# A fused layer-norm, state-space and Mish feed-forward block on one core: a new order of work, a rotation-table scan, one activation per tile and one weight ring

## The chip, the cores and the metric

The kernel runs on one core of one Trainium2 chip. The time is the device time of that core in microseconds (us), and lower is better. An execution is "fast" when it lies within 1.5% of the fastest of the same kernel, "slow" when it lies above, and "unknown" when there is only one run to judge by. The engines are called PE (TensorE, matmuls), PEld (its weight loads), DVE (VectorE), ACT (ScalarE), POOL (GpSimd) and SP (SyncE, which issues most of the transfers).

## The reference

The input is 2048 rows of 1024 bf16 numbers. The rows are normalised, and the result goes through two branches, which are added to the input.

```python
xn = _layernorm(x)                               # x: 2048 x 1024
# branch A: a diagonal complex recurrence over the rows, P = 1024 states
Lam_bar = jnp.exp(dt * Lam)
B_bar = ((Lam_bar - 1.0) / Lam)[:, None] * Bmat
Bu = jnp.einsum("bld,pd->blp", x + 0j, B_bar)
for t in range(L):
    h = Lam_bar[None, :] * h + Bu[:, t, :]
y = 2.0 * jnp.einsum("blp,dp->bld", hseq, Cmat).real + x * Dskip
# branch B: a feed-forward layer, F = 3584
h = jnp.einsum("bsd,df->bsf", x, w1) + b1
act = h * jnp.tanh(softplus(h))                  # Mish  (softplus is written out in the original)
B = jnp.einsum("bsf,fd->bsd", act, w2)
return x + A(xn) + B(xn)
```

Both kernels work on four blocks of 512 rows. A block has four stages on PE: B (the real and imaginary parts of Bu, 128 matmuls), FFN1 (224), FFN2 (224) and C (128). Every matmul has a 128x128 stationary operand and 512 columns. This makes 704 matmuls per block and 2816 in all, in both kernels. The recurrence itself runs on DVE, with one "scan unit" for each of eight groups of 128 states.

## The kernel before

Its activation takes three passes on ACT, a bias add on DVE before them and a product on POOL after them.

```python
def ffn1_block(c_, pump=None, ln_rts=()):
    for f in range(NF):                          # 28 tiles
        ...                                      # 8 matmuls into banks[bank]
        vop(lambda e, ...: e.tensor_scalar(hb[:, hs, :], banks[bank][:, :], b1col[:, f:f + 1], None, op0=ALU.add), ...)
        if pump is not None:
            ...                                  # block 0: the next pieces of the V tables, on DVE
        aop(lambda e, ...: e.activation(actT[:, f, :], hb[:, hs, :], AF.Exp), ...)
        if f % GRP == GRP - 1 or f == NF - 1:
            ...                                  # AF.Ln for all tiles of the group, then for each of them:
            aop(lambda e, ff=ff: e.activation(actT[:, ff, :], actT[:, ff, :], AF.Tanh), ...)
            pop(lambda e, ...: e.tensor_tensor(actT[:, ff, :], hb[:, hs2, :], actT[:, ff, :], op=ALU.mult), ...)
```

The end of a block makes the residual on POOL, from x and xn that are fetched again from DRAM through four buffers (NXT = 4), while the scan runs on DVE:

```python
def tail_block(c_):
    for j in range(NJ):
        scan_unit(c_, j)                         # 2 scans, carry, 6 bf16 products and sums of 128x512
    for u in range(NU):                          # 8 output tiles
        dma_unit_tiles(c_, u)                    # xtf <- x, xntf <- xn_scr, buffer u % NXT
        xdsk_prep(u)                             # POOL: xdsk = xntf * dsk, then xdsk += xtf
    ...                                          # FFN2, then C with C transposed afresh (dma_rs) in every block
    if c_ + 1 < NB:
        dma_xnT(c_ + 1)                          # 8 transposing loads from xn_scr
    for u in range(NU):
        vop(lambda e, ...: e.tensor_tensor(outs[:, os_, :], banks[u][:, :], xdsk[:, u, :], op=ALU.add), ...)
        ...
```

The start is layer norm of four row tiles, a write of xn to DRAM, eight transposing loads of it, then W1 and the sixteen transposes of B, all on SP's queue. The main loop does B first.

```python
for rt in range(min(NQ, NRT)):
    ln_tile(rt)                                  # load x, normalise, write xn_scr
dma_xnT(0)
for g in range(min(NW1S, NFG)):
    dma_w1(0, g)
for ci, Bsrc in enumerate([A_B_re, A_B_im]):
    for k in range(NK):
        ...                                      # dma_start_transpose(BT[:, ci, k, :], ...)
...
for c_ in range(NB):
    ...
    but_block(c_)                                # stage B
    ...
    ffn1_block(c_, ...)
    ...
    tail_block(c_)                               # scan, residual, FFN2, C, output
```

Of the kernel before, what the change touches and what calls it, by code (L numbers as in the profile page):

```python
# [166 lines left out]

def bass_parallel_sum__ssm_conv_s5__dense_activation_mish__prompt_kernel(
    nc: bass.Bass,
    A_x: bass.AP,  # L170
    A_Lambda_re: bass.AP,
    A_Lambda_im: bass.AP,
    A_B_re: bass.AP,
    A_B_im: bass.AP,
    A_C_re: bass.AP,
    A_C_im: bass.AP,
    A_log_dt: bass.AP,
    A_Dskip: bass.AP,
    B_x: bass.AP,
    B_w1: bass.AP,  # L180
    B_b1: bass.AP,
    B_w2: bass.AP,
    out: bass.AP,
):
    build_kernel(nc, A_x, A_Lambda_re, A_Lambda_im, A_B_re, A_B_im, A_C_re, A_C_im,
                 A_log_dt, A_Dskip, B_w1, B_b1, B_w2, out)


def build_kernel(nc, A_x, A_Lambda_re, A_Lambda_im, A_B_re, A_B_im, A_C_re, A_C_im,
                 A_log_dt, A_Dskip, B_w1, B_b1, B_w2, out, GRP=7, HBR=14):  # L190
    bf16, f32, i32 = DT.bfloat16, DT.float32, DT.int32
    assert len(A_x.shape) == 3 and len(out.shape) == 3
# [4 lines left out]
    assert S % TB == 0 and D % TB == 0 and Pch % P128 == 0 and F % 256 == 0  # L197
    NB = S // TB
    NK = D // P128
    NJ = Pch // P128  # L200
    NF = F // P128
    NFG = NF // 2
    NQ = TB // P128
    NBH = D // TB
    NU = NQ * NBH
    assert NU <= 8
    NRT = S // P128
    NST = D // 512
    GRP = min(GRP, NF)
    HBR = max(GRP, min(HBR, NF))  # L210
    EPS = 1e-5
    TTAB = TB
    LOGT = int(round(math.log2(TTAB)))
    assert (1 << LOGT) == TTAB

    def xrows(r0, nrows):
        return A_x[0, r0:r0 + nrows, :]
# [6 lines left out]

    def dsem(name, nper=1):
        return DmaSem(nc, name, nper)

    final_sem_totals = []

    xn_scr = nc.dram_tensor("bass_xn_scratch", (S, D), bf16).ap()  # L230
# [3 lines left out]

    actT = sb("actT", [P128, NF, TB], bf16); b_act = [Buf("act%d" % f) for f in range(NF)]
    hb = sb("hb", [P128, HBR, TB], bf16); b_hb = [Buf("hb%d" % i) for i in range(HBR)]
    hT = sb("hT", [P128, 2, NJ, TB], bf16); b_hT = [Buf("hT%d" % j) for j in range(NJ)]
    mtmp = sb("mtmp", [P128, 2, TTAB], bf16); b_m = [Buf("m%d" % k) for k in range(2)]
    cum = sb("cum", [P128, 2, TTAB], bf16); b_cum = [Buf("cum%d" % k) for k in range(2)]
    NW2S = 3  # L240
    w2s = sb("w2s", [P128, NW2S, 2, D], bf16); b_w2s = [Buf("w2s%d" % i) for i in range(NW2S)]
    NRS = 4
    rhs = sb("rhs", [P128, NRS, 2, D], bf16); b_rhs = [Buf("rhs%d" % i) for i in range(NRS)]
    NXD = 8
    xdsk = sb("xdsk", [P128, NXD, TB], bf16); b_xdsk = [Buf("xdsk%d" % i) for i in range(NXD)]
    NXT = 4
    xtf = sb("xtf", [P128, NXT, TB], bf16); b_xtf = [Buf("xtf%d" % i) for i in range(NXT)]
    xntf = sb("xntf", [P128, NXT, TB], bf16); b_xntf = [Buf("xntf%d" % i) for i in range(NXT)]
    NOS = 4
    outs = sb("outs", [P128, NOS, TB], bf16); b_outs = [Buf("outs%d" % i) for i in range(NOS)]  # L250
    BT = sb("BT", [P128, 2, NK, Pch], bf16); b_BT = Buf("BT")
    xnT = sb("xnT", [P128, NK, TB], bf16); b_xnT = Buf("xnT")
    Wt = sb("Wt", [P128, 2, NJ, TTAB], bf16)
    Vt = sb("Vt", [P128, 2, NJ, TTAB], bf16)
    b_tab = Buf("tab")
    NW1S = 3
    w1s = sb("w1s", [P128, NW1S, NK, 256], bf16); b_w1s = [Buf("w1s%d" % i) for i in range(NW1S)]
    if NF * TB >= 4 * D:
        upa = D // TB
        xl = nc.alloc_sbuf_tensor_at("xl", [P128, 2, D], bf16, offset=nc.lookup_mloc(actT).addr)  # L260
        xnl = nc.alloc_sbuf_tensor_at("xnl", [P128, 2, D], bf16, offset=nc.lookup_mloc(actT).addr + 2 * D * 2)
        b_xl = [Buf("xl%d" % i, shadows=[b_act[u] for u in range(upa * i, upa * (i + 1))]) for i in range(2)]
        b_xnl = [Buf("xnl%d" % i, shadows=[b_act[u] for u in range(2 * upa + upa * i, 2 * upa + upa * (i + 1))]) for i in range(2)]
    else:
        xl = sb("xl", [P128, 2, D], bf16); b_xl = [Buf("xl%d" % i) for i in range(2)]
        xnl = sb("xnl", [P128, 2, D], bf16); b_xnl = [Buf("xnl%d" % i) for i in range(2)]
    stats = sb("stats", [P128, 2, NST, 6], f32); b_stats = [Buf("stats%d" % i) for i in range(2)]
    mv = sb("mv", [P128, 2, 2], f32); b_mv = [Buf("mv%d" % i) for i in range(2)]
    rstd = sb("rstd", [P128, 2, 1], f32); b_rstd = [Buf("rstd%d" % i) for i in range(2)]
    rstd_t = sb("rstd_t", [P128, 2, 4], f32); b_rstd_t = [Buf("rstdt%d" % i) for i in range(2)]  # L270
    dsk = sb("dsk", [P128, D], bf16); b_dsk = Buf("dsk")
    zeros = sb("zeros", [P128, TTAB], bf16); b_zeros = Buf("zeros")
    b1bf = sb("b1bf", [P128, NF], bf16); b_b1bf = Buf("b1bf")
    b1col = sb("b1col", [P128, NF], f32); b_b1col = Buf("b1col")
    lam_bf = sb("lam_bf", [P128, 3, NJ], bf16); b_lambf = Buf("lambf")
    CSN_MAIN = ["lre", "lim", "ldt", "dt", "a", "th", "up2", "up3", "na", "mag", "scol", "ccol",
                "lamre", "lamim", "m512", "nre", "den", "inv", "cre2", "cim2", "ncim2", "t1", "t2",
                "mure", "muim", "nmuim", "spare"]
    NCS = len(CSN_MAIN)
    cs = sb("cs", [P128, NCS, NJ], f32)  # L280
    b_cs = [Buf("cs%d" % i) for i in range(NCS)]
    qb = sb("qb", [P128, 2, 2, NJ], f32); b_qb = [[Buf("qb%d_%d" % (i, k)) for k in range(2)] for i in range(2)]
    consts = sb("consts", [P128, 4], f32); b_consts = Buf("consts")
    up = sb("up", [P128, 2, LOGT + 1, NJ], f32)
    b_up = [[Buf("up%d_%d" % (i, k)) for k in range(2)] for i in range(LOGT + 1)]
    regA_off = nc.lookup_mloc(hT).addr
    regA_end = nc.lookup_mloc(cum).addr + 2 * TTAB * 2
    regB_off = nc.lookup_mloc(w2s).addr
    regB_end = nc.lookup_mloc(outs).addr + NOS * TB * 2
    tg_f32 = NJ * TTAB * 4  # L290
    tg_b16 = NJ * TTAB * 2
    needA = tg_f32 // 2 + tg_b16 + 2 * TTAB * 4
    needB = 2 * tg_f32 + tg_b16 + 2 * TTAB * 4
    aliased = (regA_off + needA <= regA_end) and (regB_off + needB <= regB_end)
    offA = [regA_off]
    offB = [regB_off]
    tmp_ix = [0]

    def take(shape, dtype, nbytes, reg):
        tmp_ix[0] += 1  # L300
        if aliased:
            t = nc.alloc_sbuf_tensor_at("tmp_%d" % tmp_ix[0], shape, dtype, offset=reg[0])
            reg[0] += nbytes
            return t
        return sb("tmp_%d" % tmp_ix[0], shape, dtype)
    p_tt = take([P128, NJ, TTAB // 2], f32, tg_f32 // 2, offA)
    mag_w = take([P128, NJ, TTAB], bf16, tg_b16, offA)
    iota_i = take([P128, TTAB], i32, TTAB * 4, offA)
    iot = take([P128, TTAB], f32, TTAB * 4, offA)
    p_re = take([P128, NJ, TTAB], f32, tg_f32, offB)  # L310
    p_im = take([P128, NJ, TTAB], f32, tg_f32, offB)
    mag_v = take([P128, NJ, TTAB], bf16, tg_b16, offB)
    tv1 = take([P128, TTAB], f32, TTAB * 4, offB)
    tv2 = take([P128, TTAB], f32, TTAB * 4, offB)
    if aliased:
        assert offA[0] <= regA_end and offB[0] <= regB_end
    mln_alias = (NXD * TB >= 4 * D) and (2 * NXT * TB >= 4 * D)
    if mln_alias:
        xl4 = nc.alloc_sbuf_tensor_at("xl4", [P128, 4, D], bf16, offset=nc.lookup_mloc(xdsk).addr)
        xnl4 = nc.alloc_sbuf_tensor_at("xnl4", [P128, 4, D], bf16, offset=nc.lookup_mloc(xtf).addr)  # L320
        assert nc.lookup_mloc(xntf).addr == nc.lookup_mloc(xtf).addr + NXT * TB * 2
        upd = D // TB
        b_xl4 = [Buf("xl4_%d" % i, shadows=[b_xdsk[u] for u in range(upd * i, upd * (i + 1))]) for i in range(4)]
        xx = b_xtf + b_xntf
        b_xnl4 = [Buf("xnl4_%d" % i, shadows=[xx[u] for u in range(upd * i, upd * (i + 1))]) for i in range(4)]
    else:
        xl4 = sb("xl4", [P128, 4, D], bf16)
        xnl4 = sb("xnl4", [P128, 4, D], bf16)
        b_xl4 = [Buf("xl4_%d" % i) for i in range(4)]
        b_xnl4 = [Buf("xnl4_%d" % i) for i in range(4)]  # L330
# [18 lines left out]
    def c(n):  # L349
        return cs[:, CSN[n], :]  # L350

# [568 lines left out]
```

## Time and profile before

| | before |
|---|---|
| median of the first three runs | 782.53 us (780.72 to 789.05) |
| span of the profiled run, mean granted PE clock | 777.7 us, 0.968 |
| first counted matmul starts / last matmul ends | 76.84 / 764.1 us |
| 2816 matmuls at the uninterrupted pace (below) | 608.0 us |

The page of the profile gives the busy time of each engine first, then the busy tenths of 40 equal slices, and in its fourth part the shares of the chain that ended last.

```profile
PE 627.5 (81%) x2760; PEld 277.6 (36%) x2816; DVE 568.8 (73%) x1018; ACT 261.0 (34%) x415; POOL 274.0 (35%) x276
...
PE   0000999567998699898999787999999699999992
...
PE 26%; DVE 22%; DMA 16%; POOL 14%; ACT 12%; SPq 5%; issue 4%; POOLq 0%; DVEq 0%; ACTq 0%
```

PE is the busiest engine, but its row has four empty slices at the start and holes between the blocks, and the chain that ended last runs through PE for only a quarter of the span. The other engines take turns at holding PE up. The waits say where (consumer, producer, us in total, times, longest):

```profile
POOL xdsk L634 <- DMA xntf<-bass_xn_scratch: 104.1, 32, 5.4
PE bank L761 <- DMA BT<-in_A_B_im_dram: 76.8, 1, 76.8
...
DVE outs L825 <- POOL xdsk L637: 28.8, 5, 8.2
...
PE bank L714 <- DVE hb L719: 18.3, 12, 4.5
...
PE bank L761 <- DVE outs L825: 13.2, 4, 7.0
...
PE bank L818 <- DVE hT L691: 8.6, 4, 3.3
```

PE's own lines are the 76.8 us for B at the start, 18.3 for the bias add `hb`, 13.2 for the output add and 8.6 for the scan. POOL's 104.1 us is not time lost in itself. It matters because the chain "residual fetch, POOL product, output add, free bank, next block's first matmul" is closed through it.

PE's timeline gives the same in order (start, length, engine, line, tile, count, and in brackets the idle time before it and what ended it):

```profile
76.84 29.22 PE L761 MATMUL bank<-xnT,BT 128*128 128x512 bf16 x126 [76.84 <-DMA BT<-in_A_B_im_dram]
...
145.55 1.89 PE L714 MATMUL bank<-xnT,w1s 128*128 128x512 bf16 x8 [2.52 <-DVE hb L719]
...
173.38 12.94 PE L801 MATMUL bank<-w2s,actT 128*128 128x512 bf16 x47 [6.08 <-issue]
190.27 40.87 PE L801 MATMUL bank<-w2s,actT 128*128 128x512 bf16 x173 [3.95 <-DMA w2s<-in_B_w_dram]
...
402.69 27.79 PE L818 MATMUL bank<-rhs,hT 128*128 128x512 bf16 x125
```

The line at 402.69 is a stage of 128 matmuls without an interruption (three records are missing). It shows 27.79 us. The Trainium skill ("TensorE: Matmul & The Clock Gate", Back-to-back issue gap) gives N/2.4 + 2.5 ns for a single matmul at the warm clock, which is 215.8 ns at N = 512.

### The profile page before, as it was taken

To read this page: it belongs to the slowest core of one execution; us is meant where nothing else is said; L and a number is where in the kernel's file an instruction comes from. 1 tells how busy PE (TensorE), PEld (TensorE's weight loads), DVE (VectorE), ACT (ScalarE), POOL (GpSimd) and SP (SyncE) were. 2 spreads that over 40 slices of the span, in tenths; PEclk is the share of its full clock that TensorE was granted. 3 is DMA by queue.
4 is the path that set the end of the run, shared out by engine and by line. 5 is a ranking of instruction groups with operands and counts; after the bars stand their busy time and mean duration, and the time that the engine had idled before them with its cause. 6 is when DMAs were issued, how large, how long until landed. Compare 5 with 4: busy or idle time off the path is not lost.

```text
span 777.7 us, 8473 instructions
## 1 busy us (share of the span) xinstructions
PE 627.5 (81%) x2760; PEld 277.6 (36%) x2816; DVE 568.8 (73%) x1018; ACT 261.0 (34%) x415; POOL 274.0 (35%) x276
## 2 busy tenths in 40 slices
PE   0000999567998699898999787999999699999992
PEld 0000444223443244343444333444444244444441
DVE  2599999960599879738997289549995198479932
ACT  0250004599000000799400000999100005994000
POOL 0000000546344410146745310345664300567653
PEclk9999999997999899999999989999999999999997
DMA  4279014268568761454569913354669804514372
GB/s 55 75 176 168 0 55 139 79 189 191 194 228 180 150 142 55 136 148 123 181 216 171 211 62 108 110 152 145 206 171 179 169 8 137 160 60 172 116 144 81
DMA packets 193019, 105.70 MB, mean 136 GB/s; under 512 B 112464, under 2 KB 173904, under 8 KB 192976
## 3 DMA queue, kind: packets, MB, share of 16 engines
q1 hardware_dynamic: 183376, 86.28, 44.3%
q0 software_dynamic: 4992, 14.69, 6.9%
q10 hardware_dynamic: 4608, 4.20, 1.9%
q8 instruction: 23, 0.38, 0.2%
q14 instruction: 20, 0.16, 0.1%
HBM read 71.58 MB, written 8.39 MB: 103 GB/s over the span
## 4 chain that ended last, share of the span: by engine, by line
PE 26%; DVE 22%; DMA 16%; POOL 14%; ACT 12%; SPq 5%; issue 4%; POOLq 0%; DVEq 0%; ACTq 0%
PE bank L714 15%; DMA xntf<-bass_xn_scratch 11%; PE bank L761 8%; ACT actT L737 4%; POOL xdsk L634 4%; POOL actT L739 4%; POOL xdsk L637 4%; ACT actT L732 3%; SPq L473 3%; ACT actT L727 2%; DVE stats L590 2%; PE bank L801 2%; DVE hb L719 2%; DMA xl<-in_A_x_dram 2%; POOL xtf L626 2%
## 5 line engine op out<-in xcount | busy, mean ns | idle before, releaser
L739 POOL TENSOR_TENSOR actT<-hb,actT 128x512 bf16<-128x512 bf16 x112 | 141.8, 1301 | 357.3 <-ACT actT L737 324.2
L801 PE MATMUL bank<-w2s,actT 128*128 128x512 bf16 x880 | 199.7, 386 | 15.5 <-issue 6.1
L714 PE MATMUL bank<-xnT,w1s 128*128 128x512 bf16 x876 | 196.3, 381 | 19.3 <-DVE hb L719 18.3
L761 PE MATMUL bank<-xnT,BT 128*128 128x512 bf16 x504 | 117.8, 394 | 92.6 <-DMA BT<-in_A_B_im_dram 76.8
L727 ACT ACTIVATE actT<-hb 128x512 bf16<-128x512 bf16 x112 | 62.8, 618 | 330.2 <-DVE hb L719 329.7
L801 PEld LDWEIGHTS bank<-w2s,actT 128*128 128x128 bf16 x896 | 88.5, 99 | 126.4 <-issue 17.6
L714 PEld LDWEIGHTS bank<-xnT,w1s 128*128 128x128 bf16 x896 | 87.1, 98 | 127.9 <-issue 21.3
L719 DVE TENSOR_SCALAR hb<-bank,b1col 128x512 bf16<-128x512 f32 x112 | 81.0, 747 | 58.4 <-PE bank L714 40.6
L818 PE MATMUL bank<-rhs,hT 128*128 128x512 bf16 x500 | 115.5, 389 | 9.2 <-DVE hT L691 8.6
L761 PEld LDWEIGHTS bank<-xnT,BT 128*128 128x128 bf16 x512 | 51.1, 101 | 158.6 <-DMA BT<-in_A_B_im_dram 76.8
L634 POOL TENSOR_TENSOR xdsk<-xntf,dsk 128x512 bf16<-128x512 bf16 x32 | 42.5, 1328 | 104.1 <-DMA xntf<-bass_xn_scratch 104.1
L818 PEld LDWEIGHTS bank<-rhs,hT 128*128 128x128 bf16 x512 | 50.8, 100 | 73.2 <-DVE hT L691 10.6
L825 DVE TENSOR_TENSOR outs<-bank,xdsk 128x512 bf16<-128x512 f32 x32 | 20.9, 687 | 71.0 <-PE bank L818 32.0
L732 ACT ACTIVATE actT<-actT,consts 128x512 bf16<-128x512 bf16 x112 | 70.3, 708 | 0.2
L737 ACT ACTIVATE actT<-actT 128x512 bf16<-128x512 bf16 x112 | 60.0, 616 | 0.2
L637 POOL TENSOR_TENSOR xdsk<-xdsk,xtf 128x512 bf16<-128x512 bf16 x32 | 41.3, 1291 | 4.6
L661 DVE TENSOR_TENSOR_SCAN cum<-zeros,qb,hT 128x512 bf16<-128x512 bf16 x24 | 40.4, 1682 | 0.0
L590 DVE BATCH_NORM_STATS2 stats<-xl_60 128x6 f32<-128x512 bf16 x24 | 16.5, 689 | 32.5 <-DMA xl_60<-in_A_x_dram 32.1
L658 DVE TENSOR_TENSOR_SCAN cum<-zeros,qb,hT 128x512 bf16<-128x512 bf16 x24 | 34.2, 1426 | 0.0
L727 ACT ACT_TABLE_LOAD x3 | 3.8, 1283 | 71.1 <-PE bank L761 71.0
L767 DVE TENSOR_TENSOR mtmp<-bank,Wt 128x512 bf16<-128x512 f32 x32 | 22.1, 690 | 3.0
L773 DVE TENSOR_TENSOR mtmp<-bank,Wt 128x512 bf16<-128x512 f32 x32 | 22.1, 692 | 1.1
(113 smaller groups left out, 481.2 us busy)
## 6 DMA issues: line engine op xcount, KB each, us to landing
w1s<-in_B_w_dram SPq DMA_DIRECT2D x56, 512.0 KB, 3.8
w2s<-in_B_w_dram SPq DMA_DIRECT2D x56, 512.0 KB, 3.7
xtf<-in_A_x_dram POOLq DMA_DIRECT2D x32, 128.0 KB, 3.4
xntf<-bass_xn_scratch POOLq DMA_DIRECT2D x32, 128.0 KB, 3.5
out_dram<-outs ACTq DMA_DIRECT2D x32, 128.0 KB, 4.1
xl_60<-in_A_x_dram POOLq DMA_DIRECT2D x12, 256.0 KB, 4.7
bass_xn_scratch<-xnl_61 POOLq DMA_DIRECT2D x12, 256.0 KB, 5.0
xl<-in_A_x_dram SPq DMA_DIRECT2D x4, 256.0 KB, 2.7
```

The lines of the kernel that those rows point to most:

```text
L634: pop(lambda e, bb_=bb_, xs=xs, u=u: e.tensor_tensor(xdsk[:, u, :], xntf[:, xs, :], dsk[:, bb_ * TB:(bb_ + 1) * TB], op=ALU.mult), reads=[ ...
L637: pop(lambda e, xs=xs, u=u: e.tensor_tensor(xdsk[:, u, :], xdsk[:, u, :], xtf[:, xs, :], op=ALU.add), reads=[b_xtf[xs], b_xdsk[u]], writes ...
L661: vop(lambda e, cim_=cim_, vim=vim, init_im=init_im: e.tensor_tensor_scan(out=cim_, data0=zeros[:], data1=vim, initial=init_im, op0=ALU.ad ...
L714: return e.matmul(banks[bank][:, :], lhsT=w1s[:, s_, k, fi * P128:(fi + 1) * P128], rhs=xnT[:, k, :], start=(k == 0), stop=(k == NK - 1))
L719: vop(lambda e, hs=hs, bank=bank, f=f: e.tensor_scalar(hb[:, hs, :], banks[bank][:, :], b1col[:, f:f + 1], None, op0=ALU.add), reads=[b_ba ...
L727: aop(lambda e, hs=hs, f=f: e.activation(actT[:, f, :], hb[:, hs, :], AF.Exp), reads=[b_hb[hs]], writes=[b_act[f]])
L732: aop(lambda e, ff=ff: e.activation(actT[:, ff, :], actT[:, ff, :], AF.Ln, bias=consts[:, 2:3], scale=1.0), reads=[b_act[ff], b_consts], w ...
L737: aop(lambda e, ff=ff: e.activation(actT[:, ff, :], actT[:, ff, :], AF.Tanh), reads=[b_act[ff]], writes=[b_act[ff]])
L739: pop(lambda e, hs2=hs2, ff=ff: e.tensor_tensor(actT[:, ff, :], hb[:, hs2, :], actT[:, ff, :], op=ALU.mult), reads=[b_hb[hs2], b_act[ff]], ...
L761: return e.matmul(banks[bk][:, :], lhsT=BT[:, ci, k, j * P128:(j + 1) * P128], rhs=xnT[:, k, :], start=(k == 0), stop=(k == NK - 1))
L801: return e.matmul(banks[u][:, :], lhsT=actT[:, f, q * P128:(q + 1) * P128], rhs=w2s[:, s_, fi, bb_ * TB:(bb_ + 1) * TB], start=first, stop ...
L818: return e.matmul(banks[u][:, :], lhsT=hT[:, ci, j, q * P128:(q + 1) * P128], rhs=rhs[:, s_, ci, bb_ * TB:(bb_ + 1) * TB], start=False, st ...
```

## The change

The intent is to let PE start early and never wait. In block 0 FFN1 goes first, because it needs only xn and W1. The norm's transposes go to PE. B and C are transposed once and kept on chip. One Mish activation, which reads PSUM and adds the bias, replaces the add, three passes and product. The scan uses a decaying scan and a rotation by tables from Sin, and the residual moves to DVE, on x that is kept on chip. W1 and W2 share one ring of large loads. The diff is a rewrite; its core, cut:

```diff
-    xn_scr = nc.dram_tensor("bass_xn_scratch", (S, D), bf16).ap()
...
+    def transpose0(r):
+        pb = psb(r)
+        for k in range(NK):
+            PE.group(lambda e, k=k: e.transpose(pb[:, k * P128:(k + 1) * P128], xn0[:, r, k * P128:(k + 1) * P128], ident[:]),
...
+        act(xnT[:, :, r * P128:(r + 1) * P128], src, AF.Copy, [b_bank[r]], [b_xnT[r]])
...
+    for r in range(NQ):
+        ln_stats(0, r)
+        ln_rstd(r, 1)
+        ln_norm(0, r, xn0[:, r, :], b_xn0[r])
+        transpose0(r)
...
+    def tab_angle(j):                        # DVE: 4 f32 operations; ACT: 2 Sin, 1 Copy
...
+    def tab_w(j):                            # DVE: 4 f32 operations and a small copy
...
+            act(actT[:, f, :], ps[:, bk, :], AF.Mish, [b_bank[bk], b_prm], [b_act[f]], bias=b1c[:, f:f + 1])
...
+    tab_angle(0)
+    tab_angle(1)
...
-        but_block(c_)
...
+            for g in range(NG):                    # block 0: FFN1 in 7 groups of 4 tiles
+                ffn1_group(cc, g, B8)
+                ring_load()
+                pop_n(bt_todo, load_bt, 3)
+                if g == 0:
+                    for j in range(NJ):
+                        tab_w(j)
+                        if j + 2 < NJ:
+                            tab_angle(j + 2)
...
+            for j in range(NJ):
+                bu_unit(j)
```

The rotation tables have to be ready before block 0's B stage. They are made after FFN1's first group in program order, on DVE, ACT or both.

## The prediction

> **What bounds the kernel now.** TensorE. The timeline of PE shows 128 matmuls of 128x512 in 27.79 us when nothing interrupts, 0.217 us each; 2816 of them are 611 us of the 777.7 us span. The rest: PE's first matmul is at 76.84 us (waits: "PE <- DMA BT 76.8"), because layer norm of four row tiles runs one DMA round trip at a time (6.8 us each), xnT returns through DRAM, and all of B is transposed; the last matmul ends at 764.1, a 13.6 us tail. Between them PE takes 687 us, 76 more than 611: waits for DVE `hb` (18.3, mostly in block 0, where table building shares DVE), for `outs` at block ends (13.2; POOL waits 104 us for xntf), for the three-pass activation at the FFN1-FFN2 seam, for the scan (8.6), and cold clock after gaps.
>
> **What the change does.**
> 1. Start: block 0's FFN1 needs only xn and W1. x loads go out at once; a tile's norm took 3.64 us (DVE's timeline, 10.26 to 13.90); in the new ACT order the next Sqrt sits behind a PSUM copy, so about 4.1. PE transposes replace the DRAM trip. First FFN1 matmul at 24 us: -53.
> 2. One Mish per tile, from PSUM with bias: estimate 0.7 us (a 128x512 ACTIVATE took 0.62 to 0.71), against three passes, a 0.75 us DVE add and a 1.3 us POOL product. PE makes a tile in 1.74 us. The seam and `hb` waits go.
> 3. C stays on chip (64 transposes become 16); POOL idles. bf16 products on DVE took 0.425 us without POOL, up to 0.9 beside it, so scans fall from 8 to 5 us per unit and end before FFN2 does.
> 4. New cost: rotation tables on DVE during block 0's FFN1. From before's f32 durations (tensor_scalar 0.505, scalar_tensor_tensor 0.85) one j costs 5.9 us with semaphores. The order of instructions shows ACT runs six Sin/Copy groups between Mish of group 0 and of group 1. DVE finishes its angles near 70 us, so Mish of group 1 comes near 74; PE has eight banks, does groups 0 to 2 by 47, then waits: a 25 to 30 us stall. This gives back half of point 1.
> 5. bu stage: DVE two 1.22 (1024 f32) plus two 0.425 is 3.3 us against PE 3.47: no stall. Ring: 1 MB per 7 us group, 150 GB/s, two groups of lead; before's slices show up to 228.
>
> **Sum.** 24 start + 611 + 27 stall + 3 cold + 3 small waits + 7 tail = 675; timed runs lie about 3 above the profiled span: **678 us**, range 660 to 702. Faster by over 2%: 0.98; within: 0.015; slower: 0.005.
>
> **What would show it.** PE's timeline: first FFN1 matmul at 22 to 28 us; one gap near 45 to 75 us, released by ACT (Mish); from block 1 on 153 us per block, gaps under 3 us; DVE's tables about 43 us between 30 and 75; POOL nearly zero; granted clock above 0.97 after the stall. The Trainium skill ("TensorE: Matmul & The Clock Gate", The HAM clock gate) says an idle PE falls to half clock and needs about 3.4 us of work to return; before agrees: after the 76.8 us wait 126 matmuls took 29.22 us, not 27.8.
>
> **What would make it wrong.** B's or C's transposes (1.3 us of issue each) sharing SP's queue with the ring, so PE waits for ring loads; slow SBUF-to-SBUF transposes before each block; Mish or reversed operands dearer than assumed; table loads between Sqrt and Copy; or ACT less blocked by tables than I count (then 650 to 660).

## The result, and the profile after

| | before | after |
|---|---|---|
| median of 4 runs | 782.45 us (780.72 to 789.05) | 661.71 us (660.22 to 661.99) |
| ratio of fast runs | 1 | 0.8481, 95% interval 0.8436 to 0.8526 |
| span of the profiled run, mean PE clock | 777.7 us, 0.968 | 660.2 us, 0.968 |
| first FFN1 or B matmul starts / last matmul ends | 76.84 / 764.1 us | 23.33 / 656.82 us |

A ratio is the mean time of one kernel's fast runs over the mean of the other's of the same rounds, so it is not quite the ratio of the medians quoted. The page after:

```profile
PE 617.8 (94%) x2802; PEld 281.1 (43%) x2859; DVE 371.8 (56%) x637; ACT 117.1 (18%) x163; POOL 2.7 (0%) x12
...
PE   3680999999999999999999999999999999999997
...
PE 93%; issue 4%; DMA 1%; DVE 1%; ACT 1%; ACTq 0%; POOLq 0%
```

PE's row has one hole, in the fourth slice, and none after it. The chain is 93% PE. POOL's 274.0 us became 2.7, and ACT's 261.0 became 117.1. PE's timeline has the detail:

```profile
23.33 2.72 PE L485 MATMUL ps<-xnT,ring 128*128 128x512 bf16 x6 [1.16 <-issue]
26.27 20.24 PE L485 MATMUL ps<-xnT,ring 128*128 128x512 bf16 x88 [0.22 <-issue]
66.92 4.43 PE L485 MATMUL ps<-xnT,ring 128*128 128x512 bf16 x10 [20.41 <-issue]
...
97.22 27.79 PE L494 MATMUL ps<-xnT,BT 128*128 128x512 bf16 x126
...
629.03 27.79 PE L565 MATMUL ps<-CT,hT 128*128 128x512 bf16 x125
```

FFN1 starts at 23.33 instead of waiting until 76.84 for B. There is one gap of 20.41 us. From 97.22 to 656.82 (629.03 + 27.79) PE takes 559.6 us for the remaining 2592 matmuls, which is 2592 x 0.2159: no small waits at all. After the gap ten matmuls took 4.43 us, about twice 0.216 each. This agrees with the half clock after idleness that the prediction cites from the Trainium skill ("TensorE: Matmul & The Clock Gate", The HAM clock gate).

The profile names "issue" as what ended the 20.41 us gap. ACT's timeline shows what PE really waited for, a bank that only a Mish frees:

```profile
37.40 2.42 ACT L291 ACTIVATE actT<-ps,prm 128x512 bf16<-128x512 f32 x4
39.85 1.28 ACT L291 ACT_TABLE_LOAD   x1
41.14 0.73 ACT L291 ACTIVATE cs_t<-f_t,cst 128x512 f32<-128x512 f32 x1
...
57.38 0.72 ACT L291 ACTIVATE cs_t<-f_t,cst 128x512 f32<-128x512 f32 x1 [2.19 <-DVE f_t L288]
...
62.19 0.72 ACT L291 ACTIVATE cs_t<-f_t,cst 128x512 f32<-128x512 f32 x1 [2.19 <-DVE f_t L288]
...
64.83 1.28 ACT L291 ACT_TABLE_LOAD   x1
66.13 5.31 ACT L291 ACTIVATE actT<-ps,prm 128x512 bf16<-128x512 f32 x9
```

Four Mish of group 0 run, then six table units, and the Mish of group 1 starts only at 66.13. PE resumes 0.79 us later. ACT executes in program order and waits for DVE's angle (2.19 us each time), so the pace of the tables is DVE's: 62.19 - 57.38 = 4.81 us per unit.

Two windows of the span (length, then busy time and count of PE, PEld, DVE, ACT and POOL, granted clock, DMA share, GB/s) compare block 0's FFN1 with a whole later block:

```profile
23.30:97.20 73.90, 52.86 (x219) 23.14 (x225) 45.31 (x102) 44.44 (x60) 0.00 (x0) 0.83 0.55 143
200.80:352.80 152.00, 151.21 (x691) 68.90 (x705) 82.81 (x135) 22.01 (x31) 0.00 (x0) 1.00 0.38 118
```

The later block takes 152.0 us, its matmuls alone. Block 0's FFN1 takes 73.9 us for 224 matmuls that need 48.4: 20.4 us of gap and a remainder of 5.1 us (73.9 - 48.4 - 20.4), which is put down to the cold clock: the granted clock of this window is 0.83, that of the later block 1.00.

The 117.5 us between the two spans split so. The start gave 53.5 (76.84 - 23.33). Between the first and last matmul it was 53.8 (764.1 - 76.84 is 687.3; 656.82 - 23.33 is 633.5). The tail after the last matmul gave 10.2 (13.6 - 3.4).

### The profile page after: what moved, and what is told of

Same layout as the page of the kernel before. It is cut to its first block, busy times and chain, and to the rows that moved or that the text cites. A ratio compares the mean times of both kernels' runs of the same rounds, so it can differ in the third digit from the quotient of the medians.

```text
span 660.2 us, 6994 instructions
## 1 busy us (share of the span) xinstructions
PE 617.8 (94%) x2802; PEld 281.1 (43%) x2859; DVE 371.8 (56%) x637; ACT 117.1 (18%) x163; POOL 2.7 (0%) x12
## 4 chain that ended last, share of the span: by engine, by line
PE 93%; issue 4%; DMA 1%; DVE 1%; ACT 1%; ACTq 0%; POOLq 0%
PE ps L485 30%; PE ps L551 29%; PE ps L494 17%; PE ps L565 17%; DMA prm_in<-in_B_b_dram 1%; PE ps L412 1%; ACT xnT L291 0%; DMA out_dram<-outs 0%; DVE xn_58 L285 0%; DVE rs L279 0%; ACTq L354 0%; ACTq L300 0%; DVE outs L279 0%; DVE rs L395 0%; DVE rs L285 0%
## 5 line engine op out<-in xcount | busy, mean ns | idle before, releaser
L485 PE MATMUL ps<-xnT,ring 128*128 128x512 bf16 x877 | 197.8, 385 | 22.9 <-issue 22.0
L551 PE MATMUL ps<-ring,actT 128*128 128x512 bf16 x878 | 192.9, 379 | 0.9
L485 PEld LDWEIGHTS ps<-xnT,ring 128*128 128x128 bf16 x896 | 88.8, 99 | 131.2 <-issue 28.3
L551 PEld LDWEIGHTS ps<-ring,actT 128*128 128x128 bf16 x896 | 87.7, 98 | 105.7
L494 PE MATMUL ps<-xnT,BT 128*128 128x512 bf16 x503 | 110.7, 379 | 0.5
L565 PE MATMUL ps<-CT,hT 128*128 128x512 bf16 x501 | 110.6, 379 | 0.6
L291 ACT ACTIVATE actT<-ps,prm 128x512 bf16<-128x512 f32 x112 | 75.8, 689 | 181.4 <-PE ps L485 181.3
L279 DVE TENSOR_TENSOR mt<-ps,Wt 128x1024 bf16<-128x1024 f32 x64 | 75.4, 1220 | 44.7 <-PE ps L494 44.7
L508 DVE TENSOR_TENSOR_SCAN gt<-sc,qc,hT 128x512 bf16<-128x512 f32 x48 | 61.5, 1281 | 0.8
L279 DVE TENSOR_TENSOR hT<-mt 128x512 bf16<-128x512 bf16 x128 | 53.9, 421 | 2.2
L291 ACT ACT_TABLE_LOAD x12 | 15.4, 1283 | 182.8 <-DVE outs L279 179.3
```

The source lines that it names most:

```text
L279: vop(lambda e: e.tensor_tensor(o, a, b, op=op), reads=r, writes=w)
L291: aop(lambda e: e.activation(o, a, f, **kw), reads=r, writes=w)
L485: PE.group(lambda e, k=k, fi=fi, bk=bk: e.matmul(ps[:, bk, :], lhsT=v[:, k, fi * P128:(fi + 1) * P128], rhs=xnT[:, k, :], start=(k == 0), ...
L494: PE.group(lambda e, ci=ci, k=k: e.matmul(ps[:, b0 + ci, :], lhsT=BT[:, ci, k, j * P128:(j + 1) * P128], rhs=xnT[:, k, :], start=(k == 0), ...
L508: vop(lambda e, ci=ci, init=init: e.tensor_tensor_scan(out=gt[:, i, ci, :], data0=cj("mag", j).to_broadcast([P128, TB]), data1=hT[:, j, ci ...
L551: PE.group(lambda e, f=f, fi=fi, q=q, hf=hf, bk=bk: e.matmul(ps[:, bk, :], lhsT=actT[:, f, q * P128:(q + 1) * P128], rhs=v[:, fi, hf * 512 ...
```

## The experiments

Twelve runs were made, in three sets, each on one chip beside the kernel before. All gave a correct result. Ratios are against the kernel before of the same set, whose medians (of all executions) were 774.86, 779.32 and 778.11 us. The first set is `b_mish`, `b_resid`, `b_ffn1first` and `a_pairs`, the second `a_head`, `a_warm`, `a_pairs_warm` and `a_pairs_head`, the third the rest. The changed kernel (661.71 us, 0.8481) was not run again beside them. The kernel before varies by 1% and more between executions (769.40 to 781.12 us in the first two sets, slow ones left out), so ratios of different sets cannot be told apart by less than about 1%: `a_warm` has a higher ratio than the changed kernel, and a lower median. Small differences between the `a_` runs are therefore read from medians and checked on the traces, where the start of block 0's B stage moves by nearly the same amount.

| run | kernel | median us | ratio, 95% interval |
|---|---|---|---|
| b_mish | before + one Mish per tile | 722.36 | 0.9283 (0.9206 to 0.9360) |
| b_resid | before + residual fetched early | 765.40 | 0.9858 (0.9806 to 0.9910) |
| b_ffn1first | before + FFN1 first in block 0 | 761.46 | 0.9798 (0.9734 to 0.9862) |
| b_mish_first | before + Mish + FFN1 first | 699.18 | 0.9003 (0.8957 to 0.9050) |
| a_pool | after + 60 unused POOL products | 703.37 | 0.9054 (0.9000 to 0.9109) |
| a_head | after + batched norm at the start | 656.29 | 0.8464 (0.8425 to 0.8503) |
| a_warm | after + dummy matmuls at the start | 660.03 | 0.8513 (0.8468 to 0.8557) |
| a_pairs | after + tables in pairs | 637.94 | 0.8216 (0.8174 to 0.8258) |
| a_pairs_warm | a_pairs + a_warm | 635.83 | 0.8199 (0.8161 to 0.8236) |
| a_pairs_head | a_pairs + a_head | 632.26 | 0.8154 (0.8116 to 0.8191) |
| a_best | all, and two copies moved to DVE | 630.03 | 0.8112 (0.8080 to 0.8145) |

Two theories stood against each other on where the 117.5 us came from. In the first, the parts work each in their own place: the activation is worth its waits, the early FFN1 its head start, and the residual its block ends. In the rival, the activation alone carries most of what lies between the first and last matmul, because without its POOL products the scan and residual fit as they are.

### One Mish alone, in the kernel before

```diff
-            vop(... e.tensor_scalar(hb[:, hs, :], banks[bank][:, :], b1col[:, f:f + 1], None, op0=ALU.add), ...)
-            aop(... AF.Exp ...);  aop(... AF.Ln ...);  aop(... AF.Tanh ...);  pop(... hb * actT ...)
+            aop(lambda e, bank=bank, f=f: e.activation(actT[:, f, :], banks[bank][:, :], AF.Mish, bias=b1col[:, f:f + 1]),
+                reads=[b_bank[bank], b_b1col], writes=[b_act[f]])
```

> The kernel before, with one change: each FFN1 tile leaves PSUM through one Mish activation; the DVE bias add, Ln, Tanh and the POOL product are gone. Everything else is as before (B first, residual re-read from DRAM, C streamed). Theory: most of what PE lost between its first and last matmul before (687 us for 608 us of matmuls) came from this three-engine activation: in block 0 DVE had to add biases beside table building, and in blocks 1 to 3 the POOL products came ahead of the residual chain in POOL's order, so the outputs were evacuated late. So the time falls to 705 to 725 us, PE's first matmul stays near 77 us, and the waits of DVE outs for POOL xdsk (28.8 us before) nearly vanish. Rival: the loss is spread over separate causes (residual trips, C streaming, scan arithmetic), and Mish alone wins less than 30 us (755 or more).

The median was 722.36 us of four runs (718.33, 718.47 and 726.26, and one slow run of 808.23, which was the profiled one at a clock of 0.858). The expectation held. The old scan, the old residual and the old order are all still there, and yet almost half of the gain is made (7.2 of 15.2%). The run does not tell apart the DVE add, the ACT passes and the POOL product that the Mish replaced. Because the profile of this run was slow, the same kernel was run again for a look, in the third set.

> The kernel before with one Mish per tile again, for a profile in the fast state (that of the first run fell in the slow one): about 720 us, PE's first matmul near 76 us, blocks 1 to 3 without a PE gap over 2 us, one group of gaps at the seam of FFN1 and FFN2 in block 0 where the W2 loads wait for the tables.

It took 726.06 us (one run, so its state is unknown), and its span was 724.3. PE's timeline:

```profile
105.18 48.51 PE L714 MATMUL bank<-xnT,w1s 128*128 128x512 bf16 x224
...
184.18 40.34 PE L788 MATMUL bank<-w2s,actT 128*128 128x512 bf16 x176 [11.67 <-DMA w2s<-in_B_w_dram]
224.36 27.79 PE L805 MATMUL bank<-rhs,hT 128*128 128x512 bf16 x128
255.14 27.80 PE L748 MATMUL bank<-xnT,BT 128*128 128x512 bf16 x128 [3.00 <-DMA xnT<-bass_xn_scratch]
```

FFN1 of block 0 now runs its 224 matmuls in 48.51 us without a wait, although DVE still makes the V tables beside it. In the kernel before the same stage ran from 105.90 to 167.30. The C stage of block 0 (224.36) no longer waits for the scan. In the later blocks only waits of 3.00, 0.73 and 3.67 us for xnT are left. Two of these are above the 2 us that I had set as the limit, so that detail missed slightly. The new seam at W2 (11.67 us in place of 3.95) is one thing that the Mish does not repair. From first to last matmul this run takes 642.6 us (718.4 - 75.76), against 687.3 before and 633.5 after. So the Mish alone makes 44.7 of the 53.8 us between the first and the last matmul, and of the two theories above it is the rival that was right.

### The residual fetched early, in the kernel before

```diff
-    NXT = 4
+    NXT = 8
...
         for u in range(NU):
             dma_unit_tiles(c_, u)
+        for u in range(NU):
             xdsk_prep(u)
```

> The kernel before, with the residual's tiles fetched into eight buffers ahead of the eight products, instead of one fetch, one product at a time. Theory: the chain of eight DMA round trips on POOL (about 6 us each) holds the output evacuation at the end of each block and in the tail; with it overlapped the block-end gaps of PE (5.8 and 7.3 us, plus cold clock after them) and part of the 13.6 us tail go: 762 to 770 us. Rival (POOL's late start after the 28 activation products is what holds the outputs, not the round trips): within 5 us of before, 777 or more.

The median was 765.40 us, inside the expected range (which was set from 782 us; against the kernel before of the same set it is 9.5 us), but the profile shows that two effects were added up. The gaps at the block ends and more than half of the tail went (the last matmul ended at 757.7 of a 763.6 us span, so the tail fell from 13.6 to about 6). In exchange POOL's residual products now ran all at once beside the scans, and PE waited longer for the scan: 21.5 us in total for `hT`, against 8.6 before. PE's timeline of this run:

```profile
243.77 5.17 PE L819 MATMUL bank<-rhs,hT 128*128 128x512 bf16 x16 [7.99 <-DVE hT L691]
...
435.35 3.63 PE L819 MATMUL bank<-rhs,hT 128*128 128x512 bf16 x15 [1.87 <-DVE hT L691]
```

So part of the wait at the block ends came back as a wait in the C stage. This is why an expected range that is met does not by itself prove the mechanism that was given for it.

### FFN1 first in block 0, in the kernel before

```diff
-        but_block(c_)
+        if c_ > 0:
+            but_block(c_)
...
             ffn1_block(c_, pump=(deferred, npf))
+            but_block(c_)
```

> The kernel before, with only the order of block 0 changed: FFN1 first, B after it. Theory: the order by itself is worth nothing, because the evacuation of FFN1 still sits on DVE behind the table chain (until about 90 us) and the scans, which take 8 us a unit there, start later: PE begins near 48 us instead of 77, stops after eight tiles until DVE is free, and later waits about 20 us for the scans at the C stage: 778 to 802 us. Rival: FFN1 first is where the start's gain comes from, so the time falls by 15 us or more, to 767 or less.

The median was 761.46 us: my own theory missed by at least 16 us, and the rival's "767 or less" was right (its "15 us or more" was not quite: the kernel before of this set took 774.86, so the fall is 13.4). PE's timeline:

```profile
51.28 12.28 PE L714 MATMUL bank<-xnT,w1s 128*128 128x512 bf16 x48 [51.28 <-DMA w1s<-in_B_w_dram]
79.22 0.61 PE L714 MATMUL bank<-xnT,w1s 128*128 128x512 bf16 x1 [15.67 <-DMA w1s<-in_B_w_dram]
...
222.74 27.79 PE L818 MATMUL bank<-rhs,hT 128*128 128x512 bf16 x125
```

PE started 25.6 us earlier and gave 15.67 of it back, because the W1 loads after the first three (six tiles, the 48 matmuls of the first line) queue behind B's sixteen transposes. What I had forecast as the second loss, a wait for the scan in the C stage, did not come: the stage at 222.74 has no gap. I had overlooked that the C stage takes one scan unit after the other, so it does not have to wait until all eight are done. The scans also had a longer lead: by DVE's timeline the first starts at 187.14, 35.6 us before this stage, in the kernel before at 214.36, 16.6 us before it. And I had overlooked that moving the B stage next to FFN2 also removed the waits of 6.08 and 3.95 us at that seam (new ones of 3.39 and 2.66 us, for DVE's work on the B stage, came in their place).

### Mish and FFN1 first together

> The kernel before with one Mish per tile and FFN1 first in block 0. Theory: with the evacuation on ACT the new order is worth more than the 13 us it won alone, but W1 tiles still queue behind B's 16 transposes (PE waits until about 79 us after six tiles) and the scans of block 0, at about 8 us a unit, end after FFN2, so PE waits at the C stage: 700 to 712 us against about 720. Rival: order and Mish gains overlap fully: 716 or more.

The median was 699.18 us, just below the range. The C-stage wait that my forecast contained was again not there. A scan unit took 6.89 us here. PE's timeline shows the W1 loads still behind B's transposes, with a wait of the same size as in the run before:

```profile
78.50 39.58 PE L714 MATMUL bank<-xnT,w1s 128*128 128x512 bf16 x176 [15.48 <-DMA w1s<-in_B_w_dram]
```

From this run to the changed kernel 37.5 us of span remain (697.7 - 660.2). The earlier start gives 27.6 of them (50.95 - 23.33), the time between first and last matmul 7.4 (640.9 against 633.5), and the tail 2.5 (5.9 against 3.4). No run takes apart what makes the start 27.6 us earlier: the loads of x at once, the transposes on PE in place of the trip through DRAM, or the order of the loads of W1.

### The table gap: the same tables, in pairs

```diff
-                if g == 0:
-                    for j in range(NJ):
+                if g in (1, 3, 5):
+                    for j in (g - 1, g):
                         tab_w(j)
-                        if j + 2 < NJ:
-                            tab_angle(j + 2)
+                        tab_angle(j + 2)
...
+                if g == 6:
+                    tab_w(6)
+                    tab_w(7)
```

The residual of block 0 is moved in the same way, to two tiles after groups 3 and 5. The work is the same, plus four more table loads on ACT.

> The changed kernel, with the same table work in another order: two tables after each second FFN1 group (after groups 1, 3, 5, the last two after 6) instead of all six after group 0. Four more table loads on ACT, nothing removed. Theory: PE's 20.4 us gap in block 0 is an effect of ACT's program order (Mish of group 1 behind six table groups that DVE feeds at 4.8 us each), so the gap and the cold clock after it go: 637 to 644 us, no PE gap over 2 us after the first FFN1 matmul. Rival: the table work itself is what block 0 has no room for, and the gap only moves or splits: 652 us or more.

The median was 637.94 us, as expected. PE's timeline:

```profile
25.92 47.29 PE L485 MATMUL ps<-xnT,ring 128*128 128x512 bf16 x213 [0.22 <-issue]
73.04 27.79 PE L494 MATMUL ps<-xnT,BT 128*128 128x512 bf16 x126
```

The gap is gone, and the B stage starts at 73.04 instead of 97.22. So the same tables make no wait when they stand elsewhere in ACT's order. (The residual, which was moved too, cannot have been the cause: in the changed kernel it ran on DVE from 67.67 on, after the gap.) What the tables cost sets only how long PE waits when they do stand in the way, as the next run shows.

### POOL work beside the tables

This run asks whether the emptied POOL is what makes DVE fast in the changed kernel. It adds 60 products on POOL, which feed nothing, while the tables are made.

```diff
+    pop(lambda e: e.memset(pdm[:], 0.0), reads=[b_prm], writes=[b_pdm])
+    for _ in range(60):
+        pop(lambda e: e.tensor_tensor(pdm[:, 1, :], pdm[:, 0, :], pdm[:, 0, :], op=ALU.mult), ...)
```

> The changed kernel with 60 products of 128x512 bf16 on POOL while DVE builds the tables; they feed nothing. Theory: beside POOL an f32 DVE operation on SBUF slows as before's trace shows (scalar_tensor_tensor 0.69 to 1.52 us, tensor_scalar 0.48 to 0.71), so a table takes about 9 us instead of 4.8 and PE's gap grows by 20 to 35 us: 680 to 697. Blocks 1 to 3 stay at 152 us. Rival: DVE and POOL do not disturb each other, the 0.85 us mean that my prediction used came from the form of those instructions: 660 to 664.

The median was 703.37 us, more than the 680 to 697 expected. The span was 42.1 us above that of the changed kernel (702.3 against 660.2). The direction was right and the size was not. DVE's timeline of the changed kernel, then DVE's, POOL's and PE's of this run, show the same operations and, in the last line, the second gap (the second view is of 53.2 to 60 us, PE's line of the whole):

```profile
60.43 0.48 DVE L285 TENSOR_SCALAR rr_t<-iot,sc 128x512 f32<-128x512 f32 x1
...
61.40 0.75 DVE L288 SCALAR_TENSOR_TENSOR f_t<-iot,sc,rr_t 128x512 f32<-128x512 f32 x1
...
62.80 0.16 DVE L471 COPY mu<-cs_t 128x2 f32<-128x2 f32 x1
```

```profile
52.80 7.93 POOL L429 TENSOR_TENSOR pdm<-pdm 128x512 bf16<-128x512 bf16 x6
...
53.19 1.26 DVE L286 TENSOR_SCALAR rr_t<-iot,sc 128x512 f32<-128x512 f32 x1
...
55.66 1.41 DVE L289 SCALAR_TENSOR_TENSOR f_t<-iot,sc,rr_t 128x512 f32<-128x512 f32 x1
...
58.44 1.00 DVE L475 COPY mu<-cs_t 128x2 f32<-128x2 f32 x1
...
59.35 0.47 DVE L284 TENSOR_SCALAR q_t<-cs_t,sc 128x512 f32<-128x512 f32 x1
```

```profile
109.14 30.39 PE L489 MATMUL ps<-xnT,ring 128*128 128x512 bf16 x128 [47.99 <-issue]
```

Three of these operations take about double or more, even the copy of two columns. The one right after the copy stays at 0.47. I had assumed 0.71 us for the single-input operation, and it took 1.26. The unit of one table grew from 4.8 to 10.6 us, and PE's gaps grew from 20.41 us to 11.51 and 47.99, or by 39.1 in all. A part of this that I had not counted arose before the first table: it starts at 37.30 instead of 29.18, because the small operations that prepare it slowed as well. Later blocks, with POOL idle again, still took 152.0 us each. The Trainium skill ("Advanced Engine Details and Errata", VectorE Performance Modes, Mode Summary) says that the second Vector port to SBUF is shared with GpSimd, so that GpSimd instructions and Vector instructions that use both ports block each other. The runs are consistent with it for the single-input f32 operations, the copy among them (which mode an operation runs in is not in the trace). The quoted note does not speak of the two-input operation, which slows as well (0.75 to 1.41); other passages of the skill do name that case. The trace fits two engines that hold each other up in turn: the six products of the first line take 1.32 us each, and of the seven DVE operations that start during them each starts within one product and ends after it, but for the one of 0.47 us (by the single records; POOL's are rough). So much of an operation's longer time looks like waiting.

The kernel before has the same effect in its own trace. DVE's timeline, in the first line without and in the last beside a POOL product, which is in between:

```profile
118.27 0.69 DVE L571 SCALAR_TENSOR_TENSOR Vt<-tmp_59,tmp_57 128x512 bf16<-128x512 f32 x1
...
138.36 5.83 POOL L739 TENSOR_TENSOR actT<-hb,actT 128x512 bf16<-128x512 bf16 x4 [135.91 <-ACT actT L737]
138.81 1.52 DVE L571 SCALAR_TENSOR_TENSOR Vt<-tmp_59,tmp_57 128x512 bf16<-128x512 f32 x1
```

### The head: batching the norm, and dummy matmuls

`a_head` computes the statistics of all four tiles first and takes one Sqrt of four columns.

```diff
     for r in range(NQ):
         ln_stats(0, r)
-        ln_rstd(r, 1)
+    ln_rstd(0, NQ)
+    for r in range(NQ):
         ln_norm(0, r, xn0[:, r, :], b_xn0[r])
         transpose0(r)
```

> The changed kernel, with the start's layer norm batched: statistics of all four row tiles, one Sqrt of four columns, then the four normalizations, instead of tile by tile (where the Sqrt of the next tile waits on ACT behind the PSUM copy of the last). Theory: the first FFN1 matmul comes near 18.5 us instead of 23.3; the table chain starts after the last PSUM copy, so it and PE's gap shift as a whole: about 5 us less than the changed kernel, 656 to 658. Rival: the start does not matter because the gap in block 0 absorbs it: no change (660 to 662).

It took 656.29 us, as expected: FFN1 began at 18.20 instead of 23.33, and the gap moved with it, so the total fell by about as much. PE's timeline:

```profile
61.77 4.42 PE L486 MATMUL ps<-xnT,ring 128*128 128x512 bf16 x10 [21.65 <-issue]
```

Without the gap the same edit has the same value:

> Tables in pairs and batched start together. Theory: both gains add, 632 to 634 us (about 5 less than the pairs alone, 637.9), no PE gap in block 0. Rival: with an earlier start PE runs into the tables again and part is lost: 635 or more.

This took 632.26 us, as expected, and 5.7 below `a_pairs` by the medians of two sets (the B stage starts at 67.33 instead of 73.04).

`a_warm` asks what the cold clock at the start costs. It adds dummy matmuls before FFN1.

```diff
-    NWARM = 10
+    NWARM = 24
...
+        nfill = 8 if r < 3 else 4
+        for i in range(nfill):
+            PE.group(lambda e: e.matmul(ps[:, 7, :], lhsT=zz[:, 0:P128], rhs=zz[:, :], start=True, stop=True), ...)
```

> The changed kernel, with PE kept busy by dummy matmuls up to the first FFN1 matmul (24 instead of 10 at the start, 8 after each of the first three transposes, 4 after the last). The first FFN1 matmuls then run at full clock: PE reaches its gap about 2.5 us earlier. Theory: the gap's end is set by the table chain on DVE and ACT, so the total does not move: within 1 us of the changed kernel (660.5 to 662.5). Rival: cold clock at the start is on the critical path: 2 to 3 us less.

> The same dummy matmuls on the version with tables in pairs, where PE has no gap that could absorb them. Theory: the 2.5 us of cold clock now count: 635 to 636 us against 637.9. Rival: the cold start costs nothing in either version: 637.5 or more.

`a_warm` took 660.03 us, just below its expected range, and its runs (659.08 to 661.24) overlap those of the changed kernel (660.22 to 661.99). PE's timeline:

```profile
65.07 29.96 PE L489 MATMUL ps<-xnT,ring 128*128 128x512 bf16 x125 [21.66 <-issue]
```

Two effects are mixed here. Eight warm transposes took 0.62 instead of 1.04 us, so the chain of tiles at the start, and with it the tables, ended earlier: FFN1 starts at 21.55 instead of 23.33, and the gap ends at 65.07 instead of 66.92. This part is kept. The faster matmuls before the gap are what the gap swallowed: it grew from 20.41 to 21.66. `a_pairs_warm` took 635.83, as expected, 2.1 us below `a_pairs`, but 1.35 of that is an earlier start too (21.63 against 22.98). So the traces agree with the theory, while the two gains alone (1.7 and 2.1 us by the medians) are too alike to show it.

### All of it

`a_best` is `a_pairs_head` with dummy matmuls at the start (24 in place of 10) and before and after the transposes, and with two of the four copies out of PSUM moved from ACT to DVE. The two changes were not run apart.

```diff
+    pe_fill(10)
     for r in range(NQ):
         ln_norm(0, r, xn0[:, r, :], b_xn0[r])
         transpose0(r)
+    pe_fill(4)
+    for r in (1, 3):
+        vop(lambda e, r=r: e.tensor_copy(xnT[:, :, r * P128:(r + 1) * P128], psb(r).rearrange(...)), ...)
```

> The version with tables in pairs and batched start, plus dummy matmuls that keep PE warm up to the first FFN1 matmul, plus two of the four PSUM copies of the start on DVE instead of ACT. Theory: in the version without them the 32 transposes ran at half clock (3.6 us) and the four copies in a row on ACT (3.8 us) set the first FFN1 matmul at 17.95 us; now about 16.5: 629.5 to 631.5 us against 632.3. Rival: DVE's extra 2 us of copies delay the tables, and nothing is gained: 632 or more.

It took 630.03 us (629.83 to 630.09), as expected, and beats both kernels: 4.8% below the changed one by the medians (of two sets). Its mean clock was 1.000. PE's timeline of `a_pairs_head`, then of `a_best`:

```profile
13.00 3.60 PE L412 MATMUL ps<-ident,xn 128*128 128x128 bf16 x32 [2.35 <-DVE xn L285]
```

```profile
13.19 1.99 PE L417 MATMUL ps<-ident,xn 128*128 128x128 bf16 x32 [1.36 <-DVE xn L285]
16.16 13.97 PE L497 MATMUL ps<-xnT,ring 128*128 128x512 bf16 x64
```

The transposes are faster when PE was busy just before, and the first 64 matmuls of FFN1 run at full pace (13.97 us includes the latency of the last). FFN1 begins at 16.16. The span of 628.2 is that start, plus 608.0 us of matmuls, plus about 4 us. At this pace of the matmuls PE has nothing more to give here but the first 16 us and the tail.

## Why the prediction was right or wrong

The predicted time was 678 us and the measured one 661.7. The result lies inside the range of 660 to 702, but near its lower end. "Faster by over 2%" was right. The terms of the sum, with what they measured:

| term | predicted | measured | difference |
|---|---|---|---|
| start of FFN1 | 24 | 23.3 | -0.7 |
| 2816 matmuls | 611 | 608.0 | -3.0 |
| stall for the tables | 27 | 20.4 | -6.6 |
| cold clock | 3 | 5.1 | +2.1 |
| small waits | 3 | 0 | -3 |
| tail | 7 | 3.4 | -3.6 |
| timed run minus span | 3 | 1.8 | -1.2 |

The measured column is that of the profiled run, 662.0 us; the median is 661.7. The differences add up to -16.0.

1. **The start.** Right, mechanism and size: 23.33 against 24. That a stall would give back half of it was roughly right: 20.4 of 53.5 us, where 27 of 53 were forecast.
2. **The stall.** The mechanism was right, and `a_pairs` shows it: ACT's order puts six table units between the Mish of group 0 and of group 1. The mis-sized term is the cost of "one j costs 5.9 us"; a unit took 4.8. Six units at 1.1 us less are the 6.6 us of the table. About half of the 1.1 us comes from means: I had read the mean duration of f32 operations from the kernel before, where some of them ran alone (0.69 us) and some beside POOL (1.52 us), and applied this mean to a kernel whose POOL is idle. Four operations of 0.505 and four of 0.85 make 5.42 us. The other half is what I added for the copy and for semaphores: in the trace nine operations follow each other without a pause and take 4.81 us. I knew POOL's effect, and used it for the scan in point 3, but not for the tables in point 4. `a_pool` shows it in the other direction.
3. **The matmuls.** I divided 27.79 us by 128 for the pace. That length includes the latency of the last matmul. From start to start the pace is 0.2159 us, and over 2816 matmuls the mistake is 3 us.
4. **The activation.** Right in that the seam and `hb` waits go. Mish took 0.69 us, as estimated. But its weight was not told: `b_mish` shows that this one step takes the ratio to 0.928, almost half of the gain.
5. **The scan, C and the residual.** Point 3 named C on chip, a quicker scan and an idle POOL, and the scan unit did fall to 4.71 us. The runs show that the new scan was not needed for this time by itself: in `b_mish_look` the old one causes no wait on PE, and neither does it in `b_mish_first`. In both, POOL has no activation products to do beside it: in block 1 the first two units of `b_mish_first` took 5.49 and 7.01 us, those of the kernel before, beside such products, 11.27 and 9.92 (from start to start). Nor is the new scan the larger part of the quicker unit. In block 0 of `b_mish_first` an old unit took 6.89 us beside POOL's residual products, but the first one, before these began, 5.37; the new one takes 4.59 there. Early fetching of the residual alone is worth 1.4% (`b_resid`), but the waits for `outs` that it removes are almost gone in `b_mish_first` too (one of 1.07 us is left in the first block end), so the two gains don't add up. How much of the 37.5 us from `b_mish_first` to the changed kernel belongs to the scan and how much to the loads was not separated.
6. **What the ring and B's transposes might do** (my first doubt) did not occur: no matmul waits for the ring. In the old queue order it does: 15.5 us in `b_mish_first`, which is what the new order of loads avoids.
7. **The rest.** The cold clock cost 2.1 us more than forecast, the tail 3.6 and the distance of the timed run from the span 1.2 us less. No run was made on these; they are small estimates that missed. Six of the seven differences are negative, with the stall the largest, so they did not cancel; that, and not a wrong mechanism, put the result near the lower end of the range.

The path from 1 to the best is: Mish alone 0.928, with FFN1 first 0.900, the whole change 0.848, tables in pairs 0.822, batched norm 0.815, warm start and copies 0.811. The steps are measured in this order. The ratios come from different sets. In another order each step may be worth something else. The early FFN1 does not show it: it is worth 2.0% alone and 3.0% after Mish (0.9003 over 0.9283), which the intervals do not tell apart.

What stays open is why some executions of `b_mish` take 718 us and others 726, which part of the new start makes it 27.6 us earlier than that of `b_mish_first`, and by what mechanism POOL's products and DVE's operations hold each other up.

## What to carry to other kernels

An engine that works in program order, such as ACT here, should never get a long setup block between the outputs that free PE's buffers; cut it up and put each piece shortly before it is needed. Before a duration from an old trace is put into a sum, ask what ran beside it, and take the one measured under the conditions of the new schedule. Where a wait disappears, look where the freed work moved: in `b_resid` an output wait came back in part as a scan wait, and in `a_warm` faster matmuls only lengthened the gap that followed them.

## What the Trainium skill lacked or had wrong

- "TensorE: Matmul & The Clock Gate", Part 4: PE-mode transpose, says that the full clock does not engage for transposes. Here 32 transposes took 3.60 us after an idle PE and 1.99 us after dummy matmuls, so they do run at the warm clock. Whether transposes alone would warm it is not shown.
- The same page, Back-to-back issue gap, gives a sustained 131 ns per matmul at N = 512 and calls the 216 ns formula an over-count at this size. In the profile after, 2592 matmuls ran at 215.9 ns on the mean, and in the profiles before and after no two starts of such matmuls are closer than 215.
- "ScalarE: Activation LUTs", What ACT_TABLE_LOAD costs, adds a drain to the 1283 ns load and comes to some 2.66 us per switch. Here the load took 1.28 us and the next activation began 0.01 us after it (39.85 + 1.28, then 41.14). It also began 0.03 us after the Mish before it ended (37.40 + 2.42, then 39.85). The drain does not show in this trace.
- "Advanced Engine Details and Errata", VectorE Performance Modes, has no number for the interference of GpSimd (another page describes it further and names a factor, without the shapes). Here f32 operations of 128x512 went from 0.48 to 1.26 us (one input) and from 0.75 to 1.41 us (two inputs), and a copy of 128x2 from 0.16 to 1.00 us.
- No page names the Mish function (the general cost of an activation is given). Here it took 0.69 us for 128x512 from PSUM with a bias, 0.60 when they run back to back, no more than the 0.62 to 0.71 us of the three functions that it replaced.
